# q of the later steps loaded as two tokens a partition in 512-byte runs, with a new order of every engine

## The chip, the cores and the metric

The kernel runs on one core of one Trainium2 chip. The metric is the device time of one execution in microseconds (us), lower is better; times of several executions are given by their median. The engines are called TensorE (PE), VectorE (DVE), ScalarE (ACT), GpSimd (POOL) and SyncE (SP). SP does no arithmetic here; it issues most of the transfers.

## The reference

A linear attention with decay, in blocks of tokens, feeds a two-layer network with the activation h + sin(alpha h)^2 / alpha.

```
B, H, S, D = 4, 8, 768, 64
for each block b of 64 tokens:
    intra = (q_b k_b^T * Dmask) v_b          # Dmask[i, j] = lam^(i-j) where i >= j
    inter = (q_b * lam^(i+1)) kv_state
    out[b] = intra + inter
    kv_state = lam^64 * kv_state + (k_b * lam^(63-j))^T v_b
x = out as (3072 tokens, 512)
h = x @ w_in                                 # 512 x 2048
g = h + sin(alpha * h)^2 / (alpha + 1e-9)
y = g @ w_out                                # 2048 x 512
```

## The kernel before

**Tiles.** The 3072 tokens are worked off as six chunks of 512. A chunk is four attention steps t of 128 tokens (steps 0 to 23), then phase A (h = x w_in, 16 groups of four 512-column matmuls, written A0.0 to A5.15 for chunk and group of 128 features; some groups are cut in halves, h0 and h1), the activation, and phase B (g w_out, four row tiles of four pieces each, B0.0.0 to B5.3.3). In every group of A, ACT makes the sine out of PSUM (`sin`), one of ACT, DVE and POOL squares it (`sq`), and DVE forms g from square, reciprocal and PSUM (`g`). There are six PSUM banks for all this, so PE can run only a few groups ahead of DVE.

**Attention.** For step t the float32 rows of q, k, v are scaled by powers of lam or only cast to bfloat16 (`qs`, `ks`, `vs` with the step's number), transposed (`Tq`, `Tk` on PE and a copy `cT` for steps 0 to 7; one transposing transfer `DT` from SP for later steps), multiplied (`S`), masked on DVE (`mask`), multiplied with the state (`I`) and with v (`O`, which also holds the update of the state), and copied to x (`x`).

**Loads.** Steps 0 to 7 are loaded by `quad q0` and so on, 256 KB each, with two tokens a partition in runs of 512 bytes. Steps 8 to 23 are loaded in pairs: `load q4.0` brings half of steps 8 and 9, and so on up to `load q11.1`. Of these, k and v come in 64 partitions as 512 runs of 256 bytes, q in 128 partitions as 1024 runs of 256 bytes. All of these loads but k0's (ACT) are issued by SP. The eight weight blocks are issued by POOL: `w0` to `w3` are quarters of w_in (A groups 0 to 3, 4 to 7, 8 to 11, 12 to 15), `w4` to `w7` quarters of w_out.

**What sets the order.** Each operation is recorded with a tag, its buffers and its cost. `TUNE["ORDER"]` is a table with the tags of each engine in their final order, `ON` says which engine does an operation that several can do, and `GATE` holds a transfer back until a named operation is done. Each engine works strictly in its order; a waiting instruction holds all behind it. Up to 60 us the planner puts matmuls on zeros (line 826) into the gaps that it foresees on PE.

**Names that the prediction uses.** `load_half` (lines 848 to 868) and `load_quad` (870) issue the loads, `w_block` (884) the weights, `scale` (1011), `cast` (1027) and `scale_v` (1035) are `qs`, `ks`, `vs`; line 1234 is phase A on PE, 1260 is `g`, 1313 is phase B, 1281 the last row tile, which is cut into column pieces; 1289 and 1292 are its copy out of PSUM and its store. `aeps` (969) is a small operation on alpha.

Of the kernel before, what the change touches and what calls it, by code (L numbers as in the profile page):

```python
# [5 lines left out]
ALU = mybir.AluOpType  # L6
# [22 lines left out]
    GATE={'quad q1': 'E_i0',  # L29
          'quad v2': 'ks2',  # L30
          'quad k3': 'R_f',
          'quad k4': 'cT3.0',
          'quad q4': 'cT0.0',
          'quad v4': 'g0.1h0',
          'quad k5': 'g0.8',
          'quad q6': 'Z0',
          'quad v6': 'Z5',
          'quad k7': 'B0.1.0',
          'quad q7': 'mask3',
          'quad v7': 'sq0.11',  # L40
          'load k4.0e': 'B0.3.3',
          'load v4.0': 'qs10',
          'load v4.0e': 'qs10',
          'load k5.0': 'B0.3.3',
          'load k5.0e': 'sin1.1h0',
          'load v5.0': 'sq1.8',
          'load q5.1': 'A1.0h0',
          'load v6.0': 'ks16',
          'load v6.0e': 'A2.9',
          'load k6.1e': 'g2.0',  # L50
          'load q6.1': 'S10',
          'load q7.0': 'Zs8',
          'load k7.1e': 'O11',
          'DT13': 'sin2.13',
          'load k8.0': 'o7',
          'load v8.0': 'sin2.11',
          'load k8.1': 'g2.4',
          'load k8.1e': 'A2.6',
          'DT15': 'Zs10',
          'load k9.0e': 'sq3.7',  # L60
          'load v9.1': 'Z16f',
          'load k10.0': 'B2.2.1',
          'load k10.1': 'sin2.15',
          'load v10.1': 'qs21',
          'load v10.1e': 'A3.9',
          'DT18': 'ks19',
          'DT19': 'g3.12',
          'load k11.0': 'A3.13',
          'DT23': 'A4.4'},
# [13 lines left out]
    ON={'sq2.11': 'DVE',  # L83
        'sq0.14': 'POOL',
        'sq3.0': 'DVE',
        'sq1.0h1': 'ACT',
        'sq2.4': 'ACT',
        'sq4.1': 'ACT',
        'sq2.7': 'ACT',
        'sq3.5': 'ACT',  # L90
        'sq3.14': 'ACT',
        'sq4.4': 'DVE',
        'sq5.14': 'ACT',
        'sq5.15': 'ACT',
        'qs1': 'POOL',
        'sq3.7': 'DVE',
        'sq3.15': 'DVE',
        'sq5.3': 'ACT',
        'vs8': 'POOL',
        'Zs8': 'POOL',  # L100
        'Zs10': 'POOL',
        'sq1.12': 'ACT',
        'sq2.0': 'ACT',
        'sq2.9': 'ACT',
        'sq2.14': 'ACT',
        'sq3.11': 'ACT',
        'sq4.6': 'DVE',
        'sq5.1': 'DVE',
        'qs0': 'POOL',
        'Z1f': 'ACT',  # L110
        'sq0.2h1': 'ACT',
        'sq0.4': 'ACT',
        'sq1.4h0': 'DVE',
        'qs15': 'DVE',
        'Zs14': 'DVE',
        'sq3.12': 'ACT',
        'sq3.13': 'ACT',
        'vs21': 'POOL',
        'cT0.1': 'ACT',
        'qs3': 'POOL',  # L120
        'cT3.0': 'ACT',
        'sq0.15': 'ACT',
        'vs4': 'DVE',
        'ks5': 'DVE',
        'Z6f': 'ACT',
        'qs7': 'POOL',
        'vs7': 'POOL',
        'x7': 'DVE',
        'Z7f': 'ACT',
        'vs11': 'DVE',  # L130
        'Zs17': 'DVE',
        'sq3.8': 'ACT',
        'x19': 'DVE',
        'Zs21': 'DVE',
        'sq4.15': 'DVE',
        'ks1': 'POOL',
        'ks0': 'DVE',
        'Zs1': 'ACT',
        'Zs2': 'DVE',
        'Zs3': 'DVE',  # L140
        'sq0.0h0': 'POOL',
        'sq0.7': 'ACT',
        'sq0.9': 'DVE',
# [3 lines left out]
        'cT6.1': 'ACT',  # L147
        'qs14': 'DVE',
        'x14': 'DVE',
        'sq3.4': 'DVE',  # L150
        'sq3.10': 'ACT',
        'ks20': 'DVE',
        'sq4.0': 'DVE',
        'ks21': 'DVE',
        'vs22': 'DVE',
        'sq4.8': 'ACT',
        'sq4.12': 'ACT',
        'sq5.4': 'ACT',
        'sq5.5': 'ACT',
        'o20': 'DVE',  # L160
        'o21': 'DVE',
        'Z2f': 'ACT',
        'Zi3': 'DVE',
        'sq0.0h1': 'DVE',
        'sq0.5': 'DVE',
        'sq0.8': 'POOL',
        'sq0.13': 'ACT',
        'cT4.1': 'ACT',
        'Zs4': 'POOL',
# [562 lines left out]
def bass_lightning_attn__then__act_snake_kernel(  # L732
# [10 lines left out]
    B, H, S, D = q.shape  # L743
# [3 lines left out]
    BL = 128  # L747
# [10 lines left out]
    LQW = 1.2  # L758
# [708 lines left out]
```

## Time and profile before

| | |
|---|---|
| time, median of 3 runs | 214.64 us (214.19 to 214.92) |
| the profiled execution's own time | 216.0 us |
| its span from the first to the last instruction | 214.1 us |
| busy: PE, DVE, ACT, POOL | 204.3, 140.9, 127.0, 69.3 us |
| granted TensorE clock | 1.0 in the whole span |
| read from HBM, written | 27.27 MB, 6.29 MB |

The profile lists groups of instructions by line and shape with their busy time, the mean of one, and the idle time of the engine just before them with what ended it. The timeline lists the same in order of time: start in us, length in us, engine, line, operation, output and inputs, count, and in brackets the idle time before with its releaser. Line numbers are those of the kernel before; in the changed kernel the same statements stand a few lines off (1020 is 1014 there, 1044 is 1038, 1260 is 1262).

### The profile page before, as it was taken

To read this page: it belongs to the slowest core of one execution; us is meant where nothing else is said; L and a number is where in the kernel's file an instruction comes from. 1 tells how busy PE (TensorE), PEld (TensorE's weight loads), DVE (VectorE), ACT (ScalarE), POOL (GpSimd) and SP (SyncE) were. 2 spreads that over 40 slices of the span, in tenths; PEclk is the share of its full clock that TensorE was granted. 3 is DMA by queue.
4 is the path that set the end of the run, shared out by engine and by line. 5 is a ranking of instruction groups with operands and counts; after the bars stand their busy time and mean duration, and the time that the engine had idled before them with its cause. 6 is when DMAs were issued, how large, how long until landed. Compare 5 with 4: busy or idle time off the path is not lost.

```text
span 214.1 us, 5329 instructions
## 1 busy us (share of the span) xinstructions
PE 204.3 (95%) x2216; PEld 112.8 (53%) x2216; DVE 140.9 (66%) x245; ACT 127.0 (59%) x233; POOL 69.3 (32%) x88
## 2 busy tenths in 40 slices
PE   7898999999799999999999998899999999999995
PEld 7657654657555455444455543344555444454454
DVE  2497795767789862685667866958879744355511
ACT  3662989936787337877445598624665716657411
POOL 4397129810176205654700130400411101116100
PEclk9999999999999999999999999999999999999999
DMA  6999999987998899777899889989521201050015
GB/s 178 276 256 212 216 219 275 230 184 185 200 163 179 177 191 233 142 216 164 177 161 236 179 174 186 157 196 154 123 52 49 90 11 49 2 194 3 0 63 182
DMA packets 86985, 33.90 MB, mean 158 GB/s; under 512 B 68786, under 2 KB 83506, under 8 KB 86962
## 3 DMA queue, kind: packets, MB, share of 16 engines
q1 hardware_dynamic: 79616, 22.88, 54.0%
q0 software_dynamic: 2688, 4.19, 11.1%
q10 hardware_dynamic: 4658, 6.50, 8.6%
q8 instruction: 17, 0.28, 0.5%
q14 instruction: 6, 0.05, 0.1%
HBM read 27.27 MB, written 6.29 MB: 157 GB/s over the span
## 4 chain that ended last, share of the span: by engine, by line
PE 64%; DMA 19%; DVE 6%; ACT 4%; POOL 3%; issue 2%; SPq 1%; ACTq 0%; DVEq 0%; POOLq 0%
PE M_ps L1313 30%; PE M_ps L1234 25%; DMA q<-in_q_dram 8%; DMA k<-in_k_dram 5%; DMA w<-in_moe_w_out_dram 4%; DVE gT L1260 3%; DMA alpha_sb<-in_moe_alpha_dram 3%; PE M_ps L1147 2%; POOL qk L1020 2%; PE M_ps L1281 2%; ACT t L1246 2%; PE A_ps L1096 2%; PE M_ps L1168 1%; DVE qkT L1071 1%; ACT u L1255 1%
## 5 line engine op out<-in xcount | busy, mean ns | idle before, releaser
L1234 PE MATMUL M_ps<-xT,w 128*128 128x512 bf16 (+1 forms) x424 | 88.6, 359 | 2.4 <-DVE gT L1260 2.3
L1260 DVE SCALAR_TENSOR_TENSOR gT<-u,r_sb,M_ps 128x512 bf16<-128x512 bf16 (+1 forms) x106 | 69.8, 692 | 30.1 <-POOL u L1256 15.3
L1313 PE MATMUL M_ps<-w,gT 128*128 128x512 bf16 x368 | 87.8, 380 | 1.2 <-DVE gT L1260 0.8
L1246 ACT ACTIVATE t<-M_ps,alpha_sb 128x512 bf16<-128x512 f32 (+1 forms) x106 | 65.2, 646 | 32.2 <-PE M_ps L1234 28.5
L1234 PEld LDWEIGHTS M_ps<-xT,w 128*128 128x128 bf16 x424 | 46.6, 114 | 39.0 <-DVE gT L1260 4.1
L1256 POOL TENSOR_TENSOR u<-t 128x512 bf16<-128x512 bf16 x27 | 27.9, 1041 | 86.0 <-ACT t L1246 81.9
L1313 PEld LDWEIGHTS M_ps<-w,gT 128*128 128x128 bf16 x368 | 34.1, 98 | 40.5 <-DVE gT L1260 1.8
L1255 ACT ACTIVATE u<-t 128x512 bf16<-128x512 bf16 x46 | 28.4, 628 | 0.9 <-ACT t L1246 0.2
L1020 POOL TENSOR_TENSOR qk<-q,L 128x512 bf16<-128x512 f32 x14 | 14.5, 1045 | 23.3 <-DVE qk L1020 14.8
L1188 ACT CAST xT<-M_ps 128x512 bf16<-128x512 f32 x14 | 8.1, 587 | 21.2 <-PE M_ps L1121 17.5
L1109 DVE TENSOR_TENSOR S_m<-A_ps,maskl 128x768 bf16<-128x768 f32 x16 | 15.2, 951 | 3.1 <-PE M_ps L1147 1.7
L1256 DVE TENSOR_TENSOR u<-t 128x512 bf16<-128x512 bf16 x23 | 10.1, 443 | 6.0 <-ACT t L1246 5.8
L1020 POOL TENSOR_TENSOR qk<-k,L 128x512 bf16<-128x512 f32 x9 | 9.4, 1045 | 10.6 <-DMA k<-in_k_dram 10.5
L1330 ACT COPY osb<-M_ps 128x512 f32<-128x512 f32 x13 | 7.6, 585 | 8.4 <-PE M_ps L1313 8.3
L826 PE MATMUL M_ps<-zeros 128*128 128x128 bf16 (+1 forms) x62 | 8.4, 317 | 1.2 <-DVE zeros L903 1.2
L1330 DVE COPY osb<-M_ps 128x512 f32<-128x512 f32 x7 | 4.7, 685 | 7.3 <-PE M_ps L1313 7.3
L1121 PE MATMUL M_ps<-v,qk 64*64 64x64 bf16 x320 | 8.3, 193 | 0.9 <-DVE S_m L1103 0.7
L1168 PE MATMUL M_ps<-S_m,v 64*64 64x128 bf16 (+1 forms) x384 | 9.0, 208 | 0.0
L1103 DVE TENSOR_TENSOR S_m<-A_ps,maskq 128x1024 bf16<-128x1024 f32 x6 | 7.3, 1218 | 2.1 <-PE A_ps L1096 2.1
L1020 DVE TENSOR_TENSOR qk<-k,L 128x512 bf16<-128x512 f32 x11 | 7.4, 683 | 1.8 <-DMA k<-in_k_dram 1.8
L1202 DVE TENSOR_TENSOR Zf<-M_ps,Zf 128x256 f32<-128x256 f32 x12 | 5.0, 420 | 5.4 <-ACT xT L1188 5.3
L1096 PE MATMUL A_ps<-qkT 64*64 64x128 bf16 (+1 forms) x352 | 8.2, 210 | 0.2 <-DVE qkT L1071 0.2
(72 smaller groups left out, 135.0 us busy)
## 6 DMA issues: line engine op xcount, KB each, us to landing
q<-in_q_dram SPq DMA_DIRECT2D x24, 256.0 KB, 5.4
out_dram<-osb ACTq DMA_DIRECT2D x23, 256.0 KB, 2.3
v<-in_v_dram SPq DMA_DIRECT2D x32, 128.0 KB, 4.3
k<-in_k_dram SPq DMA_DIRECT2D x32, 128.0 KB, 4.6
v<-in_v_dram SPq DMA_DIRECT2D x8, 256.0 KB, 5.4
w<-in_moe_w_in_dram POOLq DMA_DIRECT2D x4, 512.0 KB, 10.1
w<-in_moe_w_out_dram POOLq DMA_DIRECT2D x4, 512.0 KB, 10.1
k<-in_k_dram SPq DMA_DIRECT2D x7, 256.0 KB, 5.3
```

The costliest lines, as they stand in the source:

```text
L826: last = e.matmul(m_ps[i][:, 0:c], zeros[:, 0:128], zeros[:, 0:c])
L1020: rec(en, lambda e, ll=ll, xs=xs: e.tensor_tensor(o[:, :, xs], i[:, :, xs], ll, ALU.mult), *(((0.65, 0.58) if en == "DVE" else (1.04, 1.0) ...
L1096: last = e.matmul(Av[ps, h, a, ek, 0:128 - q0], T[rows, 1, a, ek, ps], T[rows, 0, a, i, q0:128])
L1109: rec("DVE", lambda e: e.tensor_tensor(S_m[jm][:, :, :].rearrange("p (a b) c -> p a (b c)", a=4)[:, :, 0:192], S_ps().rearrange("p (a b) c ...
L1168: res = e.matmul(bank(i)[64 * a:64 * a + 64, h, qs], vv[ps, h, a, ek, :], Sv[ps, h, a, ek, 0:qs.stop - qs.start], start=(op0 and i == 0 an ...
L1234: last = e.matmul(m_ps[vb.i][:, N * i:N * i + N], w1[:, kc, cols(mm)], xT[x][:, kc, ts], start=(kc == 0 and i == 0), stop=(kc == NKC - 1), ...
L1246: rec("ACT", lambda e, i=i, mm=mm: e.activation(t16[tt][:, N * i:N * i + N], m_ps[vb.i][:, N * i:N * i + N], ACTF.Sin, scale=alpha_sb[:, m ...
L1255: return e.activation(u16[tt][:, :], t16[tt][:, :], ACTF.Square)
L1256: return e.tensor_tensor(u16[tt][:, :], t16[tt][:, :], t16[tt][:, :], ALU.mult)
L1260: rec("DVE", lambda e, i=i, mm=mm: e.scalar_tensor_tensor(out=gT[g][:, mm, ts], in0=u16[tt][:, N * i:N * i + N], scalar=r_sb[:, mm:mm + 1] ...
L1313: last = e.matmul(m_ps[vb.i], gT[g][:, m, 128 * s4:128 * (s4 + 1)], w2[:, m, :], start=(m == 0 or (split and m == 8)), stop=(m == NM - 1 o ...
L1330: rec(en, lambda e: cp(e)(osb[o][:, :], m_ps[vb.i]), *((0.585, 0.48) if en == "ACT" else (0.65, 0.58)), reads=[vb.key], writes=[f"o.{o}"], ...
```

## The change

Four things change together.

1. `load q` of steps 8 to 23 puts tokens 2p and 2p+1 on partition p of a half of the partitions, as 512 runs of 512 bytes instead of 1024 runs of 256 bytes in all partitions.
2. What follows from that layout: the decay exponents of q (`E_i`, `E_f`, two additions instead of one) and the mask (`maskl`, two selects instead of one) are made for the new order of tokens; `S`, `I` and `O` of the later steps take their columns as two runs of 64 or 32 with a gap; the rows of the output tiles of chunks 2 to 5 are written to every second row of the output, 64 partitions each.
3. The tables `ORDER`, `ON` and `GATE` are replaced as a whole. They were searched again, with loads late at random in the search.
4. The planner's cost of a q load goes from 1.2 to 0.94.

```diff
-    LQW = 1.2
+    LQW, LQV = 0.94, 20.0
...
-                    a = bass.AP(q.tensor, (b * H * S + s0) * D, [[D, 128], [S * D, H], [1, D]])
-                    d = q32t[:, r0:r0 + 2, :].rearrange("p j x -> p (j x)").rearrange("p (h x) -> p h x", h=H)
-                    d = d[:, :, 64 * i:64 * i + 64]
+                    a = bass.AP(q.tensor, (b * H * S + s0) * D, [[2 * D, 64], [S * D, H], [1, 2 * D]])
+                    d = q32t[p, r0:r0 + 2, :].rearrange("p j x -> p (j x)").rearrange("p (h x) -> p h x", h=H)
...
-                        slot=f"q{n % 4}{i}", work=LQW, weight=14.3, desc=1024, tag=f"load q{n}.{i}")
+                        slot=f"q{n % 4}{i}", work=LQW, weight=LQV, desc=512, tag=f"load q{n}.{i}")
...
-            rec("DVE", lambda e: e.tensor_scalar_add(E_f[64:128, 4:4 + 2 * NB], E_f[64:128, 4:4 + 2 * NB], 64.0), 0.15,
-                reads=["E_f"], writes=["E_f4"], tag="E_f4")
+            def upper(e):
+                for lo, by in ((4, 64.0), (4 + 2 * NB, -128.0)):
+                    last = e.tensor_scalar_add(E_f[64:128, lo:lo + 2 * NB], E_f[64:128, lo:lo + 2 * NB], by)
+                return last
+            rec("DVE", upper, 0.25, reads=["E_f"], writes=["E_f4"], tag="E_f4")
...
+            def lower(e):
+                for lo, n in ((0, 64), (128, 32)):
+                    last = e.affine_select(
+                        out=maskl[0:64, lo:lo + 2 * n].rearrange("p (x b) -> p x b", x=2),
+                        in_=zeros[0:64, 0:2 * n].rearrange("p (x b) -> p x b", x=2),
+                        pattern=[[-1, 2], [-2, n]], compare_op=ALU.is_gt, fill=1.0, base=0, channel_multiplier=1)
+                return last
+            rec("POOL", lower, 0.5, reads=["zeros"], writes=["maskl"], tag="maskl1")
...
+                                    n = 32 if ek else 64
+                                    last = e.matmul(
+                                        Av[ps, h, a, ek, 0:2 * n].rearrange("p (e b) -> p e b", e=2),
+                                        T[rows, 1, a, ek, ps], T[rows, 0, a, :, 64 * i + 64 - n:64 * i + 64])
...
+                        if not op0:
+                            to, qt = to.rearrange("p (e b) -> p e b", e=2), T[rows, 0, a, :, 64 * i:64 * i + 64]
...
+                                    if ek and not op0:
+                                        to = to.rearrange("p (e b) -> p e b", e=2)[:, :, 32:64]
+                                        sm = sm[:, 0:64].rearrange("p (e b) -> p e b", e=2)
...
+                rec("ACT", lambda e: e.dma_start(
+                    out[row0:row0 + 128, :].rearrange("(p e) d -> e p d", e=2) if c > 1 else out[row0:row0 + 128, :],
+                    osb[o][:, :]),
...
     ORDER={
-           'POOL': ['E_i2', 'E_i0', 'maskq0', 'E_i1', 'R_i', 'E_i3', 'ks1', 'ident', 'aeps', 'qs1', 'qs0',
+           'POOL': ['maskq0', 'E_i0', 'E_i2', 'E_i1', 'E_i3', 'R_i', 'qs1', 'ident', 'vs1', 'w0', 'w1', 'aeps',
...
```

The order moves in all engines; three places follow. The first is POOL near the start: `aeps` (969 before, 963 now), the casts of q and k, the scaling of v, and the issues of the weight blocks (888 and 894 before, 876 and 882 now). Before:

```order
L1032 CAST qk_1<-k 128x512
L907 AFFINE_SELECT ident<-maskf 128x128
L969 TENSOR_SCALAR aeps_sb<-alpha_sb 128x16
L1032 CAST qk_1<-q 128x512
L1032 CAST qk_0<-q 128x512
L1040 TENSOR_TENSOR v_1<-v,L 128x512
L888 DMA w<-in_moe_w_in_dram 128x4x512 x3
L1032 CAST qk_3<-q 128x512
L1040 TENSOR_TENSOR v_0<-v,L 128x512
L1040 TENSOR_TENSOR v_2<-v,L 128x512
L1040 TENSOR_TENSOR v_3<-v,L 128x512
L888 DMA w<-in_moe_w_in_dram 128x4x512
```

Now:

```order
L1026 CAST qk_1<-q 128x512
L895 AFFINE_SELECT ident<-maskf 128x128
L1034 TENSOR_TENSOR v_1<-v,L 128x512
L876 DMA w<-in_moe_w_in_dram 128x4x512 x2
L963 TENSOR_SCALAR aeps_sb<-alpha_sb 128x16
L1034 TENSOR_TENSOR v_2<-v,L 128x512
L1034 TENSOR_TENSOR v_0<-v,L 128x512
L1034 TENSOR_TENSOR v_3<-v,L 128x512
L1014 TENSOR_TENSOR qk_5<-q,L 128x2x4x64
L876 DMA w<-in_moe_w_in_dram 128x4x512 x2
L882 DMA w<-in_moe_w_out_dram 128x2048 x2
```

`aeps` has moved behind the first weight blocks, and the third block of w_in now stands behind the scaling of `v_2`, `v_0`, `v_3` and of q of step 5 (`qk_5`).

The second place is DVE at the start of phase A of chunk 1: the scaling of k and q (`qk2` from `k32` or `q32`) among the `g` (writing `gT_1`, halves of 256 columns). Before:

```order
L1256 TENSOR_TENSOR u16_3<-t16_3 128x512
L1260 SCALAR_TENSOR_TENSOR gT_1<-u16_3,r_sb,M_ps 128x256
L1256 TENSOR_TENSOR u16_2<-t16_2 128x512
L1020 TENSOR_TENSOR qk2_2<-k32,L 128x2x4x64
L1260 SCALAR_TENSOR_TENSOR gT_1<-u16_3,r_sb,M_ps 128x256
L1260 SCALAR_TENSOR_TENSOR gT_1<-u16_2,r_sb,M_ps 128x256 x2
L1020 TENSOR_TENSOR qk2_3<-k32,L 128x2x4x64
L1260 SCALAR_TENSOR_TENSOR gT_1<-u16_1,r_sb,M_ps 128x256 x2
```

Now:

```order
L1014 TENSOR_TENSOR qk2_2<-q32,L 128x2x4x64
L1190 CAST xT_1<-M_ps 128x2x2x128
L1329 TENSOR_TENSOR osb_3<-osb_3,M_ps 128x512
L1262 SCALAR_TENSOR_TENSOR gT_1<-u16_2,r_sb,M_ps 128x256 x2
L1262 SCALAR_TENSOR_TENSOR gT_1<-u16_3,r_sb,M_ps 128x256 x2
L1014 TENSOR_TENSOR qk2_5<-q32,L 128x2x4x64
L1198 COPY Zf_3<-M_ps 128x128
L1262 SCALAR_TENSOR_TENSOR gT_1<-u16_1,r_sb,M_ps 128x256 x2
```

The scaling of k of steps 8 and 9 (`qk2_2`, `qk2_3` from `k32`) has left DVE for POOL; in its place stand the scaling of q of steps 8 and 11.

The third place is SP's queue where the loads of steps 8 and later begin. Before:

```order
L865 DMA v<-in_v_dram 64x8x64
L865 DMA k<-in_k_dram 64x8x64
L876 DMA v<-in_v_dram 128x4x128
L865 DMA k<-in_k_dram 64x8x64 x5
L856 DMA q<-in_q_dram 128x8x64 x3
L865 DMA v<-in_v_dram 64x8x64
L856 DMA q<-in_q_dram 128x8x64
```

Now:

```order
L853 DMA v<-in_v_dram 64x8x64
L864 DMA v<-in_v_dram 128x4x128
L844 DMA q<-in_q_dram 64x8x128 x3
L853 DMA v<-in_v_dram 64x8x64
L853 DMA k<-in_k_dram 64x8x64 x2
L844 DMA q<-in_q_dram 64x8x128
L853 DMA k<-in_k_dram 64x8x64 x4
```

The first three q loads have moved ahead of the k loads, and the fourth ahead of four of them.

More of the change, by code (lines that the diff above doesn't have):

```diff
@@ L146 @@
         'vs5': 'POOL',
[L147 to L151, printed above, removed]
         'ks20': 'DVE',
[L153 to L155 removed]
+        'sq4.0': 'ACT',
+        'vs22': 'POOL',
         'sq4.8': 'ACT',
[L157 removed]
         'sq5.4': 'ACT',
         'sq5.5': 'ACT',
[L160 to L164, printed above, removed]
         'sq0.5': 'DVE',
@@ L184 @@
         'sq1.14': 'ACT',
-        'sq1.15': 'POOL',
+        'sq1.15': 'ACT',
         'Zs11': 'DVE',
@@ L188 @@
         'sq2.10': 'ACT',
-        'vs15': 'DVE',
-        'sq2.12': 'ACT',
-        'ks17': 'DVE',
+        'vs15': 'POOL',
         'sq3.1': 'ACT',
```

253 lines of the change are left out of this document (125 added, 128 removed), and 202 rows, old and new, of the table ORDER.

## The prediction

> **What bounds the kernel now.** I read the page first, then the waits of PE, then the timeline around each wait.
>
> ```profile
> PE 204.3 (95%) x2216; PEld 112.8 (53%) x2216; DVE 140.9 (66%) x245; ACT 127.0 (59%) x233; POOL 69.3 (32%) x88
> DMA  6999999987998899777899889989521201050015
> ```
>
> PE is busy for 95% of the span, DMA for most of the first three quarters, and no other engine above 66%. So the time is PE's own work plus PE's gaps. The work is the same before and after (the same matmuls in A, B and attention), so what a new order can win lies in the gaps. The view of waits lists them:
>
> ```profile
> PE M_ps L1234 <- DVE gT L1260: 2.3, 3, 1.0
> PE M_ps L826 <- DVE zeros L903: 1.2, 1, 1.2
> PE M_ps L1313 <- DVE gT L1260: 0.8, 2, 0.5
> PE M_ps L1313 <- DMA w<-in_moe_w_out_dram: 0.4, 1, 0.4
> ```
>
> Once phase A has begun, PE waits 2.3 + 0.8 us for DVE's g and 0.4 us for a weight block: 3.5 us in all, the most that better timing can bring behind the start. The timeline shows the gaps, and the one of DVE ahead of each:
>
> ```profile
> 55.51 0.69 DVE L1020 TENSOR_TENSOR qk<-k,L 128x512 bf16<-128x512 f32 x1 [1.57 <-DMA k<-in_k_dram]
> 56.65 1.93 PE L1234 MATMUL M_ps<-xT,w 128*128 128x256 bf16 x12 [1.04 <-DVE gT L1260]
> 58.81 1.93 PE L1234 MATMUL M_ps<-xT,w 128*128 128x256 bf16 x12 [0.24 <-DVE gT L1260]
> ...
> 105.26 1.04 PE L1313 MATMUL M_ps<-w,gT 128*128 128x512 bf16 x4 [0.32 <-DVE gT L1260]
> ...
> 132.94 0.43 DVE L1044 CAST v<-v 128x512 bf16<-128x512 f32 x1 [1.76 <-issue]
> 134.07 1.92 PE L1234 MATMUL M_ps<-xT,w 128*128 128x512 bf16 x8 [0.98 <-DVE gT L1260]
> 136.47 6.22 PE L1313 MATMUL M_ps<-w,gT 128*128 128x512 bf16 x28 [0.48 <-DVE gT L1260]
> ```
>
> At 55 us DVE stands 1.57 us on the scaling of k of step 8, whose load is late; the g behind it come late, the banks stay full, and PE loses 1.04 + 0.24 us. At 131 us DVE stands 1.76 us on a cast of v (the view puts it down to no engine, and its input is a load), and PE loses 0.98 + 0.48 us. Two late loads on DVE make 2.74 of the 3.5 us. The start is the other reserve: the first group of A begins at 19.30.
>
> ```profile
> 7.72 0.26 POOL L969 TENSOR_SCALAR aeps_sb<-alpha_sb 128x16 f32<-128x16 f32 x1 [2.85 <-DMA alpha_sb<-in_moe_alpha_dram]
> 11.19 2.51 POOL L888 DMA_DIRECT2D w<-in_moe_w_in_dram  x3
> 17.26 0.81 POOL L888 DMA_DIRECT2D w<-in_moe_w_in_dram  x1
> 18.09 1.06 POOL L1020 TENSOR_TENSOR qk<-q,L 128x512 bf16<-128x512 f32 x1
> 19.30 14.20 PE L1234 MATMUL M_ps<-xT,w 128*128 128x256 bf16 x80
> ```
>
> The sixteen groups of A0 then run for 14.0 us (to 33.33, where B begins) without a gap.
>
> **The change part by part.** The sum goes against the profiled execution, 216.0 us (span 214.1 and 1.9 around it); it lies 1.36 above the median of 214.64, and I carry the difference over to the median.
>
> *The q loads.* Packet time per descriptor comes from a stretch with runs of 512 bytes on SP's queue (4 to 13 us) and the one with runs of 256 bytes (48 to 150 us):
>
> ```profile
> q1 hardware_dynamic: 4746, 2.36, 107.2%
> ...
> q1 hardware_dynamic: 63385, 15.81, 84.7%
> q10 hardware_dynamic: 1440, 2.62, 7.2%
> ...
> L856 SPq DMA_DIRECT2D q<-in_q_dram x16: 475/624/1842, 50.7 to 131.6; - x16
> L865 SPq DMA_DIRECT2D k<-in_k_dram x32: 596/635/1728, 39.8 to 142.7; - x32
> ```
>
> 9 us x 16 engines x 1.072 / 4746 is 32.5 ns for 512 bytes, 102 x 16 x 0.847 / 63385 is 21.8 ns for 256. One q load takes 64 packets an engine today, 64 x 21.8 = 1.40 us, and 32 x 32.5 = 1.04 us then. Sixteen loads save 16 x 0.36 = 5.7 us of engine time out of 102. None of this is time on PE by itself: after 150 us the DMA row falls to 1 and 2 tenths while PE goes on for 60 us, so the loads are done long before the end, and only lateness counts. The issue does not get cheaper either: SP needs 0.62 us for a q load of 1024 runs and 0.64 us for a k load of 512, so the number of runs does not set it. Value: 0 by itself, with up to 0.36 us earlier landing for what is queued directly behind a q load.
>
> The Trainium skill, "DMA: Bandwidth & Descriptors", Specifications, sets 512 bytes as the least size for line rate and some 27 GiB/s an engine; by that a run of 512 bytes would take 17.7 ns, a load 0.57 us, and the sixteen would save 13 us of engine time. The trace disagrees with 32.5 ns. The rules at that page's end ask for 128 partitions for the best bandwidth, and q now goes to 64; the trace gives no price for that alone.
>
> *Place one, DVE at 55 us.* The scaling of k of steps 8 and 9 leaves DVE; what DVE does there now is q of steps 8 and 11, whose loads SP issues ahead of the k loads. A late k now holds POOL, which is 32% busy. If q is there, both gaps go: -1.04 - 0.24 = -1.28 us. If POOL's later work (squares for the same g) is held by the late k instead, 0.
>
> *Place two, DVE at 131 us.* Of seven scalings and casts of late loads that stand on DVE among the g of chunk 3, the new table keeps four: v of steps 17, 19 and 20 and k of step 20. But it holds loads of steps 18 to 21 back behind sines of that same chunk, so this wait can come again: between -1.46 (gone) and +1.5 (a second load as late as the first). I take 0: fewer chances to wait, each with its load issued later.
>
> *The start.* `aeps` leaves the head of POOL, where alpha's late landing held the cast of q for 2.85 us. Against it, ACT now issues the load of k0 only behind a cast of k1, which needs k1's load, third in SP's queue instead of first.
>
> ```profile
> 1.31 0.43 ACTq L876 DMA_DIRECT2D k<-in_k_dram  x1
> 4.01 0.61 POOL L1032 CAST qk<-k 128x512 bf16<-128x512 f32 x1 [1.84 <-DMA k<-in_k_dram]
> ...
> k<-in_k_dram ACTq DMA_DIRECT2D x1, 256.0 KB, 4.4
> ...
> L1103 DVE TENSOR_TENSOR S_m<-A_ps,maskq 128x1024 bf16<-128x1024 f32 x6 | 7.3, 1218 | 2.1 <-PE A_ps L1096 2.1
> L1187 DVE TENSOR_TENSOR xT<-M_ps,lamX 128x512 bf16<-128x512 f32 x4 | 2.6, 679 | 0.0
> 19.60 0.68 DVE L1187 TENSOR_TENSOR xT<-M_ps,lamX 128x512 bf16<-128x512 f32 x1
> ```
>
> 512 packets take 9 / 4746 x 512 = 0.97 us by the first row of SP's queue above, so k1 lands at 4.0 + 2 x 0.97 = 5.9; its cast (0.6) ends at 6.5; k0 lands 4.4 later at 10.9. Its cast (0.6), transposes and DVE's copy (an estimate of 0.7 for both) end at 12.2. In the new order of DVE all four masks stand behind that copy, and with them four x and two short copies: 4 x 1.22 + 4 x 0.68 + 0.5 = 8.1, so the last x ends at 20.3. It ends at 19.60 + 0.68 = 20.28 today. Value 0; bounds -1.0 (k0 a microsecond earlier, nothing lost to alpha) and +1.0.
>
> *The small additions.* One more addition on DVE (0.17 us) stands where DVE waits for lam, one more select on POOL (0.29 us) while POOL is a third busy: 0, and 0.3 at most. Matmuls whose columns come in two runs have no row; the nearest is the weight read with a stride:
>
> ```profile
> L1234 PEld LDWEIGHTS M_ps<-xT,w 128*128 128x128 bf16 x424 | 46.6, 114 | 39.0 <-DVE gT L1260 4.1
> L1313 PEld LDWEIGHTS M_ps<-w,gT 128*128 128x128 bf16 x368 | 34.1, 98 | 40.5 <-DVE gT L1260 1.8
> ...
> 73.41 0.17 PE A_ps L1096 x16
> ```
>
> Strided w reads 114 ns against 98. At 16% on 640 matmuls of 0.17 / 16 us that is 1.1 us, at nothing 0; whole runs of 64 columns are nearer to contiguous, so 0.
>
> *The tail.* B's last piece is now the one of 256 columns (ACT, 128 KB) instead of 128 (DVE and SP, 64 KB).
>
> ```profile
> L1289 ACT COPY osl<-M_ps 128x256 f32<-128x256 f32 x1 | 0.4, 372 | 1.2 <-PE M_ps L1281 1.2
> L1289 DVE COPY osl<-M_ps 128x128 f32<-128x128 f32 x1 | 0.3, 292 | 2.2 <-PE M_ps L1281 2.2
> ...
> out_dram<-osl ACTq DMA_DIRECT2D x1, 128.0 KB, 1.8
> out_dram<-osl SPq DMA_DIRECT2D x1, 64.0 KB, 1.6
> ```
>
> 0.37 - 0.29 + 1.8 - 1.6 = +0.3 us.
>
> *Sum.* -1.28 + 0 + 0 + 0 + 0.3 = -1.0 us: 215.0 for a profiled execution like this one, 213.6 for the median.
>
> **The rivals.**
>
> *All late loads go.* The order was made for late loads, DMA has 5.7 us more room, and DVE's exposed scalings fall. Then 3.5 us of gaps go and the tail costs 0.3: 214.64 - 3.2 = 211.4. Against it: four operations on late loads stay on DVE at place two, and their loads are gated.
>
> *The waits only move.* POOL, held by a late k, delays squares for the same g, and place one's 1.28 us come back: 214.9.
>
> *The third weight block is late (slower).* POOL issues strictly in order. Today the third block of w_in is issued within the 2.51 us from 11.19, by 13.70. Now it stands behind three scalings of v and that of q of step 5, the thirteenth 256 KB load; today the thirteenth (q of step 4) is scaled at 18.09 to 19.15. So the block is issued at about 19.2, and lands by the rows of the weight blocks
>
> ```profile
> DMA to landing us min/median/max: 6.9/10.1/11.9
> ...
> DMA to landing us min/median/max: 5.3/10.1/14.4
> ```
>
> 5.3 to 10.1 us later, at 24.5 to 29.3. A0.9, the first group that needs it, is the eighth in PE's order: 19.3 + 7 x 14.0 / 16 = 25.4. From a landing later than 25.4 on, PE stands: 0 to 3.9 us. The lower end is for a block with little else under way, which is nearer here, since the first two blocks have by then mostly landed; but at the middle, 2.3, the time is 213.6 + 2.3 = 215.9.
>
> *q into half the partitions is slow.* If the 64 partitions took twice the packet time, sixteen loads would cost 16 x (2.08 - 1.40) = 10.9 us more of engine time where 7% of 102 are free, some 3.8 us over: 217.4. Against it: k and v, already in 64 partitions, land in about the same time as q in 128 partitions:
>
> ```profile
> q<-in_q_dram SPq DMA_DIRECT2D x24, 256.0 KB, 5.4
> v<-in_v_dram SPq DMA_DIRECT2D x32, 128.0 KB, 4.3
> ```
>
> 1.1 us less for half the packets, and 32 x 21.8 ns is 0.7.
>
> **How the numbers follow.** Chances: the forecast 0.35 (its own range 212.8 to 214.4), all waits gone 0.20, waits only moved 0.15, weight block late 0.25, half partitions 0.05. A measurement of this kernel tells about 0.3% from no change, so faster means below 214.0, slower above 215.3. Faster: 0.25 of the forecast's 0.35, the 0.20, and 0.02 of the moved waits, 0.47. Same: 0.10 of the forecast and 0.09 of the moved waits, 0.19. Slower: 0.25, 0.05 and 0.04 of the moved waits, 0.34. The range for 8 in 10 takes in the start's -1.0 below 212 and most of the late block above: 211.0 to 216.8.
>
> **What would show it.** Right: no DVE wait on k around 55 us and PE without its 1.04; a first A group within 0.5 us of 19.3; a thirteenth load scaled near 18 and A0.9 with no wait on a weight load; SP's q loads still at 0.62 us and q packets near 32 ns. Wrong: a gap of PE between 25 and 30 us on w (the late block), long gaps on POOL at a k load followed by PE waiting for g, or a first A group later than 20.3. I would be most wrong if gaps that today do not exist, between 60 and 130 or after 140 us, open because DVE or ACT stands at some other load.

## The result, and the profile after

| | before | changed |
|---|---|---|
| time, median | 214.78 us (214.19 to 215.21, 4 runs) | 257.91 us (256.43 to 258.01, 4 runs) |
| the profiled execution: time, span | 216.0, 214.1 us | 256.43, 254.4 us |
| granted clock, mean over the span | 1.0 | 0.932 |

The ratio is 1.199, with a 95% interval of 1.194 to 1.205. The forecast was 213.6 us with a range of 211.0 to 216.8: wrong, by 44 us and in the sign. Some profiles read below were taken in the longest execution of their kernel, above all that of experiment 2 (264.91 us at a granted clock of 0.755, where its nine other executions took 213.65 to 217.47), and also those of experiments 6 (217.66 us) and 11 (215.08 us).

The page of the changed kernel, first the busy shares, then the span in 40 slices of 6.4 us:

```profile
PE 205.1 (81%) x2189; PEld 113.6 (45%) x2220; DVE 143.9 (57%) x246; ACT 124.7 (49%) x226; POOL 74.0 (29%) x96
...
PEclk9999999999999999999997999799999997995555
DMA  6999999797999999897389889001001111111111
GB/s 182 297 236 241 220 226 238 182 195 186 225 201 176 194 210 201 127 244 183 104 99 230 181 117 90 4 0 31 13 8 48 43 53 51 51 51 50 51 50 42
```

PE is as busy in microseconds as before (204.3), in a span that is 40 us longer: the time went mostly into waiting. And the last ten slices have a signature of their own. Something is moved all the time, at 42 to 53 GB/s and never more, and the DMA row stands at 1: one tenth of sixteen engines. The last ten slices of the kernel before go from 0 to 194 GB/s, in bursts with pauses between them. The stretch from 200 us to the end, in the view of transfers (packets, MB, share of 16 engines):

```profile
q10 hardware_dynamic: 1444, 2.58, 12.7%
```

12.7% is 2.03 of 16 engines, and q10 carries ACT's stores. So a store now keeps two engines busy and leaves fourteen idle. The single packets recorded in the trace say the same: from 205 to 245 us two packets of q10 are under way at a time for 87% of the stretch, each of 2 KB in 84 ns (24 GB/s); before the change (190 to 214 us) it is up to 18. At 51 GB/s a store of 256 KB takes 5.1 us. Chunks 2 to 5 write 16 tiles of 256 KB (the last in three pieces), 4.19 MB, or 82 us of two engines, one store behind the other.

Where that costs PE time is seen best against a kernel with the same loads, tables and masks, in which the copies to x put the tokens back into their natural order and each tile is stored whole (called plain stores below; span 210.1 us). Apart from the stores it differs in these copies alone, which take ACT 710 ns each instead of 587. The view of stretches, first of the changed kernel, then of the one with plain stores; columns are length, busy time of each engine, granted clock, DMA share, GB/s:

```profile
0.00:20.00 20.00, 14.52 (x304) 11.12 (x307) 12.57 (x29) 9.57 (x20) 11.84 (x24) 1.00 1.04 238
20.00:110.00 90.00, 87.73 (x1036) 50.43 (x1045) 73.86 (x129) 59.28 (x112) 38.12 (x48) 1.00 1.00 202
110.00:200.00 90.00, 79.75 (x744) 40.65 (x754) 50.91 (x80) 47.33 (x80) 22.00 (x23) 0.96 0.49 92
200.00:240.00 40.00, 23.06 (x119) 11.39 (x118) 6.55 (x11) 8.13 (x14) 2.08 (x2) 0.83 0.13 50
240.00:254.00 14.00, 0.00 (x0) 0.00 (x0) 0.00 (x0) 0.37 (x1) 0.00 (x0) 0.50 0.13 48
```

```profile
20.00:110.00 90.00, 87.82 (x1034) 50.39 (x1053) 73.99 (x129) 60.01 (x112) 38.00 (x48) 1.00 1.02 203
110.00:200.00 90.00, 88.57 (x796) 45.22 (x809) 56.86 (x88) 54.27 (x90) 24.11 (x25) 1.00 0.49 109
sum 210.00, PE 198.61 PEld 111.96 DVE 143.88 ACT 126.42 POOL 73.89; mean PE 49.65 PEld 27.99 DVE 35.97 ACT 31.60 POOL 18.47
```

From 20 to 110 us the two are alike to 0.1 us of PE. The stores in question begin at 116 us (ahead of them go the eight of chunks 0 and 1, which are stored whole). From 110 to 200 us PE of the changed kernel idles 10.3 us instead of 1.4, from 200 to 240 us 16.9, and the last 14 us are stores alone. The waits of PE name the causes:

```profile
PE A_ps L1093 <- DMA qkT<-qk: 8.4, 2, 4.2
PE M_ps L1283 <- ACT osl L1291: 4.4, 1, 4.4
PE M_ps L1236 <- ACT osb L1333: 3.8, 2, 3.4
PE M_ps L1316 <- DVE osb L1333: 3.5, 2, 3.3
```

**Loads behind stores (8.4 us).** The first row is PE waiting for transposed q and k, twice 4.2 us, and has nothing to do with stores at first sight. SP's queue shows the link. In the changed kernel:

```profile
119.11 6.13 SPq L853 DMA_DIRECT2D v<-in_v_dram  x3
125.28 2.98 SPq L853 DMA_DIRECT2D k<-in_k_dram  x1
128.31 3.52 SPq L1048 DMA_TRANSPOSE qkT<-qk  x1
```

With plain stores, the same issues in the same order:

```profile
118.87 3.19 SPq L853 DMA_DIRECT2D v<-in_v_dram  x3
122.10 0.64 SPq L853 DMA_DIRECT2D k<-in_k_dram  x1
122.78 1.35 SPq L1048 DMA_TRANSPOSE qkT<-qk  x1
```

The k load takes SP 2.98 us to issue instead of 0.64 (before, no k load took more than 1.73), and the transposing transfer is issued 5.5 us later. ACT had issued the first two rearranged stores at 116.0 and 120.3 us, 10.3 us of work for two engines. In the view of transfers from 120 to 132 us the DMA share falls to one tenth for microseconds at a time, while loads of v are under way:

```profile
DMA  6859721111793111111059411111113968991111
```

The three v loads above take 11.4 us to land (median); with plain stores the same three take 3.1:

```profile
v<-in_v_dram SPq DMA_DIRECT2D x3, 128.0 KB, 11.4
...
v<-in_v_dram SPq DMA_DIRECT2D x3, 128.0 KB, 3.1
```

The likely reading is that fourteen engines have then done their part of the load, and the load waits for the two that also carry the stores. That a load waits for its slowest engine is argued from these rows; that the plain stores take the waits away is measured. PE at the end of that chain:

```profile
134.17 0.37 PE L1093 MATMUL A_ps<-qkT 64*64 64x128 bf16 x16 [4.24 <-DMA qkT<-qk]
```

**Copies behind stores (11.7 us).** `osb` is a ring of six buffers. When the stores fall behind, the copy out of PSUM waits for a buffer, PSUM stays full, and PE stops. ACT has a second trouble: it issues the stores itself. ACT's timeline, with lines of its issues (ACTq) and of its work:

```profile
207.11 0.58 ACT L1333 COPY osb<-M_ps 128x512 f32<-128x512 f32 x1 [5.10 <-DMA out_dram<-osb]
...
224.91 5.99 ACTq L1337 DMA_DIRECT2D out_dram<-osb  x1
230.93 0.27 ACT L1291 COPY osl<-M_ps 128x128 f32<-128x128 f32 x1 [6.06 <-issue]
```

The 5.10 is a copy that waits for the buffer of an old store. The 5.99 is the issue of one store, 0.34 us before; a copy that stands behind it starts 6.06 us late, and with it the 4.39 us that PE waits on line 1283. The issue of a store, minimum, median and maximum in ns, in the changed kernel and before:

```profile
L1337 ACTq DMA_DIRECT2D out_dram<-osb x23: 338/522/5986, 55.1 to 237.0; - x23
```

```profile
L1334 ACTq DMA_DIRECT2D out_dram<-osb x23: 338/339/455, 48.7 to 209.5; - x23
```

**The tail and the clock.** PE's last matmul ends at 231.25 + 3.60 = 234.85 us, 19.6 us ahead of the end; with plain stores at 205.44 + 1.91 = 207.35, 2.8 us ahead.

```profile
231.25 3.60 PE L1283 MATMUL M_ps<-w,gT 128*128 128x256 bf16 x16 [4.39 <-ACT osl L1291]
```

```profile
205.44 1.91 PE L1287 MATMUL M_ps<-w,gT 128*128 128x256 bf16 x16
```

The same sixteen matmuls take 3.60 us instead of 1.91: from 230 us on the granted clock is 0.50. It falls three times before that, each time behind a gap of PE (4.24 us to 134.17, 4.20 to 158.94, 3.31 to 212.98). In the view of stretches:

```profile
134.40:137.90 3.50, 3.06 (x58) 1.65 (x44) 3.35 (x7) 2.01 (x4) 0.00 (x0) 0.51 1.03 208
158.30:161.70 3.40, 2.41 (x21) 1.23 (x23) 0.00 (x0) 0.35 (x1) 0.00 (x0) 0.51 0.20 43
212.90:216.40 3.50, 3.42 (x9) 1.23 (x10) 1.54 (x4) 1.95 (x3) 0.00 (x0) 0.51 0.13 51
```

Behind the gap of 3.39 us that ends at 207.75 it does not fall. In all PE is busy for 205.1 us instead of 198.6, with the same number of records. With the 3.60 us at the end, 12.5 us of PE's work lie in these stretches, of which half (6.2 us, an estimate) is the price of the clock.

So the 44.3 us between the two spans add up: 16.8 of stores behind PE's end (19.6 - 2.8), 8.4 of late transposes, 11.7 of waits for copies after 200 us (3.39 + 3.31 + 0.60 + 4.39), 6.5 of longer matmuls at the lower clock, and 0.9 in small waits.

### The profile page after: what moved, and what is told of

Its sections match the earlier page's. It is cut to its first block, busy times and chain, and to the rows that moved or that the text cites. A ratio compares the mean times of both kernels' runs of the same rounds, so it can differ in the third digit from the quotient of the medians.

```text
span 254.4 us, 5336 instructions
## 1 busy us (share of the span) xinstructions
PE 205.1 (81%) x2189; PEld 113.6 (45%) x2220; DVE 143.9 (57%) x246; ACT 124.7 (49%) x226; POOL 74.0 (29%) x96
## 3 DMA queue, kind: packets, MB, share of 16 engines
q0 software_dynamic: 2688, 4.19, 9.2%
## 4 chain that ended last, share of the span: by engine, by line
PE 55%; DMA 20%; ACTq 7%; SPq 4%; ACT 3%; POOL 2%; issue 2%; DVE 2%; DVEq 0%; POOLq 0%
PE M_ps L1236 29%; PE M_ps L1316 22%; DMA qkT<-qk 6%; ACTq L1337 5%; DMA w<-in_moe_w_in_dram 4%; DMA out_dram<-osb 4%; DMA w<-in_moe_w_out_dram 3%; SPq L853 3%; DMA v<-in_v_dram 2%; ACTq L1294 2%; ACT t L1248 2%; PE M_ps L1148 1%; PE A_ps L1093 1%; SPq L864 1%; PE M_ps L1171 1%
## 5 line engine op out<-in xcount | busy, mean ns | idle before, releaser
L1316 PE MATMUL M_ps<-w,gT 128*128 128x512 bf16 x351 | 86.0, 385 | 5.7 <-DVE osb L1333 3.5
L1258 POOL TENSOR_TENSOR u<-t 128x512 bf16<-128x512 bf16 x25 | 26.0, 1045 | 93.3 <-ACT t L1248 75.9
L1257 ACT ACTIVATE u<-t 128x512 bf16<-128x512 bf16 x43 | 26.6, 627 | 0.9
L1258 DVE TENSOR_TENSOR u<-t 128x512 bf16<-128x512 bf16 x28 | 12.9, 466 | 15.8 <-ACT t L1248 15.8
L1014 POOL TENSOR_TENSOR qk<-k,L 128x512 bf16<-128x512 f32 x15 | 15.6, 1042 | 7.1 <-PE M_ps L1119 3.3
L1093 PE MATMUL A_ps<-qkT 64*64 64x64 bf16 (+1 forms) x256 | 5.8, 210 | 8.4 <-DMA qkT<-qk 8.4
L1283 PE MATMUL M_ps<-w,gT 128*128 128x128 bf16 (+1 forms) x48 | 5.7, 286 | 5.0 <-ACT osl L1291 4.4
L1038 ACT CAST v<-v 128x512 bf16<-128x512 f32 x8 | 4.9, 614 | 8.5 <-DMA v<-in_v_dram 8.5
L1093 PEld LDWEIGHTS A_ps<-qkT 64*64 64x64 bf16 x256 | 4.1, 110 | 10.4 <-DMA qkT<-qk 8.7
L1038 POOL CAST v<-v 128x512 bf16<-128x512 f32 x7 | 4.5, 645 | 14.2 <-DMA v<-in_v_dram 13.8
```

Of the source, the lines that this page charges most:

```text
L1014: rec(en, lambda e, ll=ll, xs=xs: e.tensor_tensor(o[:, :, xs], i[:, :, xs], ll, ALU.mult), *(((0.65, 0.58) if en == "DVE" else (1.04, 1.0) ...
L1093: last = e.matmul(Av[ps, h, a, ek, 0:2 * n].rearrange("p (e b) -> p e b", e=2), T[rows, 1, a, ek, ps], T[rows, 0, a, :, 64 * i + 64 - n:64 ...
L1257: return e.activation(u16[tt][:, :], t16[tt][:, :], ACTF.Square)
L1258: return e.tensor_tensor(u16[tt][:, :], t16[tt][:, :], t16[tt][:, :], ALU.mult)
L1316: last = e.matmul(m_ps[vb.i], gT[g][:, m, 128 * s4:128 * (s4 + 1)], w2[:, m, :], start=(m == 0 or (split and m == 8)), stop=(m == NM - 1 o ...
```

## The experiments

All kernels were compared with the kernel before on the same chip, whose median there was 213.8 to 214.4 us.

**1. The stores alone.** The kernel before with the changed stores and nothing else. (The layout of q stays the old one, so the rows of the output land in another order than the reference's. The pieces of the last tile are changed likewise.)

```diff
-                rec("ACT", lambda e: e.dma_start(out[row0:row0 + 128, :], osb[o][:, :]),
+                rec("ACT", lambda e: e.dma_start(
+                    out[row0:row0 + 128, :].rearrange("(p e) d -> e p d", e=2) if c > 1 else out[row0:row0 + 128, :],
+                    osb[o][:, :]),
```

> The kernel before, order and loads untouched; only the stores of chunks 2 to 5 are written as in the change, 2 x 64 partitions to every second row (the rows of those chunks come out in another order). Theory engines: the store's outermost dimension is 2, so it runs on 2 of the 16 DMA engines and a 256 KB store takes about 5.2 us (51 GB/s in the changed kernel's last 40 us); sixteen of them behind one another make 83 us that begin near 130, so 225 to 255 us. The Trainium skill (DMA: Bandwidth & Descriptors, Why a DMA increments its semaphore by 16 and not by 1) has the number of engines as the largest up to 16 that divides the slowest dimensions of both sides, here 2. Theory rows: every second row is slow by itself; the same 225 to 255. Theory order: the new order costs the 43 us; 214.7 here.

Measured: 261.74 us, ratio 1.225 [1.216, 1.235], above the 225 to 255 that the theories engines and rows had expected. The two waits that cost most:

```profile
PE M_ps L1234 <- DVE gT L1260: 14.2, 5, 4.7
PE A_ps L1096 <- DMA qkT<-qk: 4.3, 1, 4.3
```

The stores alone cost the whole loss, and 4 us more than with the new order. DVE's late `g` take the largest place here. Behind them stands ACT, which makes some of the squares, and waits for a store's buffer or stands at a store's issue:

```profile
ACT osb L1331 <- DMA out_dram<-osb: 6.8, 1, 6.8
...
ACT u L1255 <- issue: 5.5, 1, 5.5
```

Where PE's wait shows up depends on the order; its source is the same.

**2. The same rows, two stores.** The changed kernel with each rearranged store cut in two: partitions 0 to 63 to the even rows, 64 to 127 to the odd ones.

```diff
-                rec("ACT", lambda e: e.dma_start(
-                    out[row0:row0 + 128, :].rearrange("(p e) d -> e p d", e=2) if c > 1 else out[row0:row0 + 128, :],
-                    osb[o][:, :]),
+                for z in range(2):
+                    rec("ACT", lambda e, z=z: e.dma_start(
+                        out[row0 + z:row0 + 127 + z:2, :], osb[o][64 * z:64 * z + 64, :]),
```

> The changed kernel with each permuted store given as two stores of 64 partitions, one for the even and one for the odd rows, same rows as before in the output. Theory engines: 64 divides by 16, the stores use all engines again, 213 to 217 us, and no wait of PE on a copy of osb. Theory rows: still every second row, 250 or more. Theory order: 250 or more.

Measured: 214.64 us, ratio 1.005 [1.001, 1.009]: 0.5% over the kernel before, so that nearly all of the loss is gone.

```profile
out_dram<-osb ACTq DMA_DIRECT2D x30, 128.0 KB, 2.4
```

Each half lands in 2.4 us, though it writes every second row just as the changed store does. It isn't the stride of the rows.

**3. Plain stores.** The changed kernel, in which the copy to x puts the tokens back in their natural order, so that a tile is stored whole.

```diff
+                    if not op0:
+                        o = xT[x][:, 2 * jj:2 * jj + 2, 256 * nn:256 * nn + 256].rearrange(
+                            "p h (i b y) -> p i h y b", i=2, y=2)
+                        i = M_ps[:, a:b + 1:b - a, 0:256].rearrange("p i (h y b) -> p i h y b", h=2, y=2)
...
-                rec("ACT", lambda e: e.dma_start(
-                    out[row0:row0 + 128, :].rearrange("(p e) d -> e p d", e=2) if c > 1 else out[row0:row0 + 128, :],
-                    osb[o][:, :]),
+                rec("ACT", lambda e: e.dma_start(out[row0:row0 + 128, :], osb[o][:, :]),
```

> The changed kernel, but the copies to x put the tokens of the later steps back into their natural order, and all stores are whole tiles to consecutive rows as before. Theories engines and rows: 213 to 217 us; the new order and the new loads are then seen alone, my sum has 213.6 for them, with the first group of A at 20.08 in the changed kernel instead of 19.30 rather 214.4. Theory order: 250 or more. If the copies with a step of two elements cost more than 587 ns each, it shows in the row of line 1190.

Measured: 212.7 us, ratio 0.998 [0.994, 1.002], just below the 213 to 217 expected. No wait of PE for `g` above 0.2 us is left.

**4. The loads alone.** The new loads of q with the masks and matmul columns that they need, plain stores, and the tables of the order of before.

> The new q loads, masks and matmul columns with natural rows in the stores, but the order, the engines and the gates of the kernel before. What the loads do alone: 214.7 by the prediction (value 0, at most some tenths faster), q packets near 32 ns and q landing in 4.3 us as in the changed kernel instead of 5.1. If matmuls with columns in two runs cost more, up to 1.1 us slower.

Measured: 214.4 us, ratio 1.001 [0.998, 1.004]. The wait at 55 us stays, as 0.90 us:

```profile
56.99 3.67 PE L1251 MATMUL M_ps<-xT,w 128*128 128x256 bf16 x24 [0.90 <-DVE gT L1277]
```

So the loads by themselves are worth nothing that can be measured, and the first gap belongs to the order: of eight traces with the old order seven show it, with 0.77 to 1.04 us (all but that of experiment 6, where PE had waited 2.24 us for a weight block at 50 us), of six with the new order none. A q load did not land earlier either: 5.6 us (median, 48 to 150 us) where 4.3 had been expected and 5.1 were measured before.

**5 to 7. The number of pieces, in adjacent rows.** To separate the number of pieces from the rows once more, the kernel before got stores written as 2, 4 or 16 pieces of adjacent rows: the same bytes at the same places.

```diff
-                rec("ACT", lambda e: e.dma_start(out[row0:row0 + 128, :], osb[o][:, :]),
+                rec("ACT", lambda e: e.dma_start(
+                    out[row0:row0 + 128, :].rearrange("(e p) d -> e p d", e=2) if c > 1 else out[row0:row0 + 128, :],
+                    osb[o][:, :]),
```

> The kernel before, with only the access pattern of the output stores of chunks 2 to 5 changed: the outermost dimension is now 2, but the rows stay where they were (2 x 64 x 512 with the two halves of the tile one behind the other), so the same bytes go to the same places as before. Theory engines (a store whose outermost dimension is 2 runs on two of the 16 DMA engines, whatever rows it writes): as the rearranged stores alone, 261.74 us there, so 255 to 265 us, with 50 to 54 GB/s in the last slices and a DMA row of 1 tenth. Theory rows (the loss comes from writing every second row): no change, 212.6 to 215.2 us.

> The same edit with an outermost dimension of 4. Theory engines: four engines, so twice the 51 GB/s, 102 GB/s, and 2.6 us for a store of 256 KB where two engines took 5.1. The stores of a chunk (4 x 256 KB, 10.3 us) then go into the 28 us or so that a chunk lasts until the stores gather near the end; a loss of 0 to 10 us, 214 to 224 us. Theory rows: no change, 212.6 to 215.2 us.

> The same edit with an outermost dimension of 16. Theory engines: all 16 engines, so no change, 212.6 to 215.2 us, stores landing in about 2.6 us. A third theory, that any splitting of the store's rows into two dimensions costs time: slower here too, by tens of us.

Measured: 214.38 us with 2 (ratio 1.000 [0.997, 1.004]), 215.54 with 4 (two runs, 213.41 and 217.66), 214.37 with 16 (1.001 [0.998, 1.005]). For 2, theory engines had expected 255 to 265. But the listed instructions show that these three kernels test nothing: adjacent pieces were merged back into one dimension of 128 rows when the kernel was built, and only the rearranged store kept its two.

```
2 pieces, every second row:  DMA out_dram<-osb 2x64x512
2 pieces, adjacent rows:     DMA out_dram<-osb 128x512
```

**8. The order alone.** The kernel before with the three new tables (`ORDER`, `ON`, `GATE`), and its old loads and stores.

> The kernel before (its loads of q, its masks, its stores) with the three tables of the change (order, engines, gates) alone. If the order is what closes the two gaps at 55 and 131 us: the time of the change with plain stores, 212.7 us, ratio near 0.995, no wait of PE for g over 0.3 us. If the order needs the new q loads for it (0.36 us less engine time each): some of the waits for g come back and the time is that of before, 213.8 us, ratio 1.000.

Measured: 213.16 us, ratio 0.996 [0.993, 0.999]. No wait for `g` above 0.2 us. The gain of the change, small as it is, is in the order.

**9 and 10. The number of pieces, in rows that can't be merged.** Experiment 1 with 16 pieces of eight rows, and with 4 pieces of 32. Each tile's rows land in another order than the reference's.

```diff
-                    out[row0:row0 + 128, :].rearrange("(p e) d -> e p d", e=2) if c > 1 else out[row0:row0 + 128, :],
+                    out[row0:row0 + 128, :].rearrange("(p e) d -> e p d", e=16) if c > 1 else out[row0:row0 + 128, :],
```

> The kernel before with the output stores of chunks 2 to 5 rearranged as 16 x 8 x 512: piece e of eight partitions writes every sixteenth row of the tile, which no pattern of two dimensions can tell, so that the split stays in the transfer (each tile's rows land in another order than the reference's). Theory outermost dimension (the pieces of the outermost dimension are dealt out to the DMA engines, two pieces to two engines): 16 engines, so stores of 256 KB landing in about 2.3 to 2.6 us and the time of before, 212.6 to 215.2 us. Theory strided rows (rows of a store that don't follow one another are slow): 250 us or more, as with every second row.

> The same with 4 x 32 x 512 (piece e writes every fourth row). Theory outermost dimension: four engines, 51 x 2 = 102 GB/s, some 2.6 us of transfer for a store of 256 KB and 25 GB/s an engine; the 18 stores or so of chunks 2 to 5 then take 47 us of the last 100 instead of 92, and wait little for one another: 214 to 220 us, with a few waits for a free osb buffer at the most. Theory strided rows: 250 us or more.

Measured with 16: 214.4 us, ratio 1.000 [0.997, 1.003]. A store lands in 3.0 us (2.3 before):

```profile
out_dram<-osb ACTq DMA_DIRECT2D x23, 256.0 KB, 3.0
```

Every sixteenth row is a wider stride than every second, and costs nothing: theory strided rows falls for good. Measured with 4: 230.78 us, ratio 1.077 [1.069, 1.084]. The rate while stores queue, in the view of transfers from 190 us to the end:

```profile
DMA  0003122222232220000000003122222222222221
GB/s 0 0 13 19 38 82 101 101 103 103 101 120 103 101 90 19 0 0 0 0 0 0 0 6 25 27 76 101 103 101 103 99 92 98 98 102 100 97 85 31
```

101 to 103 GB/s is twice the 51 of two pieces, as forecast: 25 GB/s for each engine. In the packets of the trace four are now mostly under way at a time (66% of 216 to 227 us), and up to 18 with sixteen pieces. The time was not as forecast (214 to 220): the stores are not spread over the chunks. Eight tiles' worth of them, 2.3 MB and 22 us of four engines, are issued from 195 us on, and 13.0 us of them lie behind PE's last matmul (it ends at 216.7 of 229.7).

**11 and 12. A head without its waits.** With plain stores PE waits 0.9 us for the identity and 0.8 us for k0 ahead of phase A. The table of the order was changed at three places:

```diff
-'alpha in', 'ks1', 'quad k0',
+'quad k0', 'alpha in', 'ks1',
-'R_i', 'qs1', 'ident',
+'R_i', 'ident', 'qs1',
-'vs3', 'qs5', 'w2', 'w3',
+'vs3', 'w2', 'w3', 'qs5',
```

> The changed kernel with plain stores (212.7 us) and three moves in the table of the order: ACT issues the load of k0 before its cast of k1 instead of behind it, POOL makes the identity before the cast of q1 instead of behind it, and issues the third and fourth blocks of w_in before the scaling of q of step 5. If the head's waits (0.95 for ident, 0.83 for ks0) delay A: the first group of A begins 0.5 to 1.5 us earlier than 19.9 and the time is 211.2 to 212.2 us. If DVE's masks and x set the start of A anyway: A begins within 0.3 us of 19.9 and the time is 212.7 us.

> The changed kernel with plain stores once more, on the chip and beside the runs of the kernel with the moved head: 212.7 us, ratio to the kernel before 0.994 to 0.998, and an interval of which the upper end lies below 1.000.

Measured: the moved head 214.52 us, ratio 0.998 [0.994, 1.001]; plain stores again 213.03 us, 0.994 [0.991, 0.998]. The move brought nothing that can be measured: the two intervals overlap, and A begins at 20.96 us in the profile of the moved head and at 20.91 in that of plain stores beside it. In the profile of experiment 3, the same kernel as the latter, A began at 19.91, so the start moves by a microsecond from one execution to another, and no time in it can be put down to the three moves. What does differ is when loads land. With the load of k0 issued at 2.13 us instead of 6.67, two loads that are needed first land later. ACT's cast of k1 and DVE's of the next q with the moved head:

```profile
7.42 0.62 ACT L1026 CAST qk<-k 128x512 bf16<-128x512 f32 x1 [5.11 <-DMA k<-in_k_dram]
...
9.71 0.43 DVE L1026 CAST qk<-q 128x512 bf16<-128x512 f32 x1 [4.70 <-DMA q<-in_q_dram]
```

and with plain stores beside it:

```profile
6.66 0.62 ACT L1026 CAST qk<-k 128x512 bf16<-128x512 f32 x1 [4.35 <-DMA k<-in_k_dram]
...
8.49 0.43 DVE L1026 CAST qk<-q 128x512 bf16<-128x512 f32 x1 [3.47 <-DMA q<-in_q_dram]
```

That the late k0 of the new order is what lets k1 and q in first is the likely reading; it is not shown, since the three moves were not tried one by one and each kernel has one trace.

The best versions are the order alone (213.16 us) and the change with plain stores (213.03 in its second series). Both are faster than the kernel before by 0.4 to 0.6% (the first series of plain stores, 0.998, could not tell), and they are not told apart here.

## Why the prediction was wrong

**The step that failed: the stores had no term.** The list of the change says that the rows of chunks 2 to 5 "are written to every second row of the output, 64 partitions each", and the sum prices one store only, in the tail: "0.37 - 0.29 + 1.8 - 1.6 = +0.3 us", for the size of B's last piece. The sixteen rearranged stores were left out of the sum, of the rivals and of the range. Each went from one outermost dimension of 128 to one of 2, from sixteen engines to two. In place of that missing term the runs showed +43 to +45 us, the changed kernel's 257.9 us against 214.6 and 212.7 with the same stores halved or undone (experiments 2 and 3); and 261.7 us with the stores alone (experiment 1).

The trace of before has no store of this form, and does not show that it goes to two engines. Given that, a bound could have been made from its page: its highest rate is 276 GB/s, 17 for each of 16 engines; two engines move 35 GB/s by that (an estimate), and 4.19 MB take 121 us where some 100 were left. Had the stores only been noticed as an unknown, the upper end of the range would have been tens of microseconds away. The Trainium skill, "DMA: Bandwidth & Descriptors", has the rule in the section on why a DMA increments its semaphore by 16: the number of engines is the largest up to 16 that divides the slowest dimensions, those of size one aside, of both access patterns. By that 2 x 64 x 512 goes to two engines, 4 x 32 x 512 to four, 16 x 8 x 512 and 64 partitions to sixteen. The runs agree in all four cases (51 GB/s with two packets under way, 102 GB/s with four, 3.0 us and 2.4 us to landing with up to 18 and 16).

The rival "q into half the partitions is slow" came near it and looked at the wrong side: it asked whether a transfer over 64 partitions is slower, and of the loads. Experiment 2 shows that stores from 64 partitions are not slow, and experiment 4 (ratio 1.001) that the loads into 64 cost nothing.

**The other terms**, read from the runs with plain stores:

| step | forecast | shown |
|---|---|---|
| place one, DVE at 55 us | -1.28 | gone with the new order; 0.90 of it stays with the old order and the new loads, 0 to 1.28 in other traces of the old order |
| q loads by themselves | 0 | ratio 1.001 [0.998, 1.004] |
| a packet of a q load | 32.5 ns | 38 ns with the new order, 43 with the old |
| SP's issue of a q load | 0.62 us, not cheaper | 0.635 us |
| place two, DVE at 131 us | 0 (-1.46 to +1.5) | gone, in both parts of the change alone: its better end (0.46 to 1.46 us in five traces of the old order and the old loads) |
| start of A | 19.30, within 1.0 | 20.08 changed, 19.91 and 20.91 with plain stores: 0.6 to 1.6 later |
| third block of w_in late | 0 to 3.9 as a rival | none above 0.2 us (0.43 with the order alone) |
| tail | +0.3 | +0.2 (2.75 us behind PE's last matmul, 2.54 before) |
| sum without the stores | -1.0 | -1.1 (212.7 to 213.78, and 213.03 to 214.12) |

That the sum without the stores agrees is in part luck: place two was worth 0.5 to 1.5 us where the sum has 0, and the late start took about as much back.

The row of q loads in the changed kernel, and PE at place one, where 57.71 now follows on the group before it without a gap:

```profile
L844 SPq DMA_DIRECT2D q<-in_q_dram x16: 604/635/1277, 45.5 to 133.9; - x16
...
53.15 4.54 PE L1236 MATMUL M_ps<-xT,w 128*128 128x256 bf16 x31
57.71 1.04 PE L1316 MATMUL M_ps<-w,gT 128*128 128x512 bf16 x4
```

The start was mis-sized in one place: the load of k0 was issued at 6.37 us, as forecast, but took 5.7 us to land instead of 4.4. So k0's cast, forecast at 10.9 us, starts at 12.1, and the chain of masks and x behind it ends at 21.4 instead of 20.3.

```profile
k<-in_k_dram ACTq DMA_DIRECT2D x1, 256.0 KB, 5.7
```

The third weight block was late, and cost next to nothing. POOL issued it at 17.50 us instead of the 19.2 of the rival, since the load of q of step 5 was scaled by then. It took 9.3 us to land, near the upper end that the rival used, and came at 26.8. Group A0.9, forecast at 25.4, was due at just that time, since A had begun late: a weight load stood 0.51 us, and PE itself shows no gap. The 0.23 us that PE did wait at 23.12 were for the second block, which is needed from the 25th matmul of A on (A0.4) and was under way from 12.22 to 23.07.

```profile
17.50 1.58 POOL L876 DMA_DIRECT2D w<-in_moe_w_in_dram  x2
...
12.22 10.85 DMA w<-in_moe_w_in_dram
...
23.12 10.79 PE L1236 MATMUL M_ps<-xT,w 128*128 128x512 bf16 x51 [0.23 <-DMA w<-in_moe_w_in_dram]
26.81 6.62 PEld L1236 LDWEIGHTS M_ps<-xT,w 128*128 128x128 bf16 x32 [0.51 <-DMA w<-in_moe_w_in_dram]
```

The 5.7 us of engine time that the longer runs should save are not seen clearly. With the new order SP's queue takes 56.4% of 211.5 us with the old loads and 54.6% of 211.0 with the new, 4.1 us less; with the old order it takes 54.0% of 214.1 and 53.6% of 212.6, 1.6 less, within what executions of one kernel differ (110.4 to 115.6 us in the traces of before and of experiments 5 to 7). The packet price was the part that was off. In the records of single packets from 48 to 150 us, a packet of 512 bytes took 37.9 ns with the new order (experiment 3) and 43.2 with the old (experiment 4), not the 32.5 of the stretch from 4 to 13 us, in which nearly all of this queue's packets are that long; one of 256 bytes took 22.0 before.

The prediction named its own weak point as "gaps that today do not exist, between 60 and 130 or after 140", at some other load. Gaps did open there, but at stores that no step had looked at.

## What to carry to other kernels

When a transfer is rewritten, look at the outermost dimension on either side before anything else: a "(p e) d -> e p d" with e of 2 is the same number of bytes and rows, and eight times fewer engines. Price every transfer of a change, the output's too, even where the change is about the loads; a bound from the page's own highest rate, divided by sixteen for one engine, is enough to see the danger. And where a steady low rate with a DMA share of 1 or 2 tenths stands at the end of a span, look for a transfer that few engines carry: here it was no limit of the memory, from and to which the same kernel moves up to 297 GB/s.

## What was not expected of the hardware

- Loads on another queue landed late while two engines carried a queue of stores: three loads of v took 11.4 us instead of 3.1 with plain stores, and SP stood 2.98 us at an issue of 0.64.
- ACT stood up to 5.99 us at the issue of a store with earlier ones still under way (before, 0.46 at most), about the 5.1 us that one store takes, with its copies behind it.
- The rate of one engine in these stores was the same with two and with four of them, 25 GB/s, so that the number of pieces scaled it: 51 and 102 GB/s.
- A packet of 512 bytes took 32.5 ns where nearly all packets of its queue were that long, and 38 to 43 ns among packets of 256 bytes.
- The granted clock fell to 0.5 behind four of PE's five gaps of 3.3 to 4.4 us, three times for 3.4 us and then to the end; that cost some 6.5 us of PE's own time on top of the waits.
